# Gate sums of an xLSTM layer in three pieces instead of four, with the third gate move an iteration later

## The chip, the cores and the metric

The kernel runs on one core of a Trainium2 chip. The metric is the device time of one execution in microseconds; the median of three runs counts. The core's engines each work through a queue of their own in order: TensorE (PE, with its weight loads as PEld), VectorE (DVE), ScalarE (ACT), GpSimd (POOL) and SyncE (SP). SP and POOL also issue DMA transfers; an instruction that waits for one holds up everything behind it on its engine.

## The reference

The layer is an xLSTM cell (4 batches, 8 heads, 768 time steps, head size 40) and behind it a mixture of eight experts, of which each token takes two. Of the cell, the gates matter here:

```
m_new  = max(f[t] + m, i[t])          # a running maximum over the time steps
f_stab = exp(f[t] + m - m_new)
i_stab = exp(i[t] - m_new);  m = m_new
C = f_stab * C + i_stab * outer(v[t], k[t])
n = f_stab * n + i_stab * k[t]
y = sigmoid(o[t]) * (C @ q[t]) / max(|n . q[t]|, 1)
```

Then `x` (3072 tokens of 320) goes through the router (`x @ w_gate` plus scaled noise, the best two of eight, softmax) and through `relu(x @ w1[e]) @ w2[e]` for its two experts, weighted and added.

## The kernel before

The cell is computed in chunks of 64 time steps. A unit `u` is one chunk of one half of the batches, 16 pairs of batch and head at once; there are 24 units, and a loop over `i` (`while i < NU - LEAD`) runs over them, with parts of units `i`, `i + 1` and `i + 2` in one turn. The names used below, with `u` in brackets:

- `e(u)` (`e_part`, L347): TensorE multiplies the operands `LE` and `RE`, which hold the gates' sums, and ScalarE takes the exponential (L350): the decay matrix `w`. A pair of units reads one of two buffers of `LE` and `RE`.
- `s(u)` (L370, L367): scores of queries and keys; VectorE multiplies them with `w` to `p(u)` (L384).
- `kd(u)` (L378, VectorE): decayed keys; `c(u)` (L399, TensorE): the state for the next unit, taken out by ScalarE (L402).
- `o(u)` (L409, TensorE): the outputs; VectorE divides (L414, L416, L420, here called the division), POOL multiplies with the o gate (L421). `t(u)` (L432) transposes the result for the router.

In turn `i` TensorE's order is `c(i)`, `o(i)`, `t(i-1)`, `e(i+2)`, `s(i+2)`; for `i` below 2 the halves of `e` stand around. VectorE's order in a turn is `kd(i+1)`, the division of `o(i)`, `p(i+1)`, then some steps of the gates' sums. At a turn's start SP and POOL issue the loads of unit `i + 3` into one of four buffers (SP: q and k, half of v, the o gates; POOL: the other half of v), and POOL the store of unit `i - 1` (L424).

The gates' sums are made by `gate_math(t0, t1)`, eight VectorE instructions per piece of time steps: the scan of the running maximum (L230), an addition and a subtraction (L233, L235), a second scan within each chunk (L240), two subtractions (L242, L244), and two writes of the rounded sums and their rests into `HL` (L247, L249). Pieces 0 to 128 and 128 to 256 are made ahead of the loop. The others come from one generator, `gates2`, of which `gates_on(n)` takes the next `n` steps: `GATES[0]` ahead of the loop, two in its preparation, and `GATES[i + 1]` at the end of turn `i`, for `i` of 0 to 5. The gates themselves come in transfers: 256 to 512 by POOL early (L219), 512 and up by SP (L801), behind the loads of units 2 and 3.

`gate_move(kk)` issues three transfers that copy the sums of 128 time steps out of `HL` into a buffer of `LE` (L258) and `RE` (L260, two). Move `kk` serves units `2 kk` and `2 kk + 1` of the first half of the batches. Moves 0 to 2 stand ahead of the loop; the others at the start of even turns, move 3 at `i = 2`, move 4 at `i = 4`, on POOL's queue while `i < XV = 13`.

## Time and profile before

| | us |
|---|---|
| median of three runs (498.49 to 502.42) | 498.79 |
| the profiled execution | 500.44 |
| its span in the trace | 498.6 |

The profiled execution lies 1.65 us above the median, and 1.84 us of it lie around the span. Times in the rows are microseconds from the span's start. A row of a timeline has start, duration, engine, line, operation and tiles; what stands in square brackets is the engine's idle time before it and what ended that. "SPq" is SP's queue of transfers, where the row tells the issue and not the landing. [...]

### The profile page before, as it was taken

The numbers are of one execution on the slowest core, as the hardware profiler recorded it, in microseconds if no ns is written. First come the engines' busy times: TensorE is split into PE (matmuls) and PEld (weight loads), VectorE is DVE, ScalarE is ACT, GpSimd is POOL, SyncE is SP. The second block draws the span as 40 slices with busy tenths as digits, with TensorE's granted clock in tenths as the row PEclk, the third lists the DMA queues.
The fourth block names the chain that finished last, engine by engine and source line by source line (L and its number), as shares of the span: only waits on it lengthen the run. The fifth ranks groups of instructions, "written<-read, shape, count | busy, mean of one in ns | idle before, by whom it ended". The sixth has DMA issues, their size and how long they took to land.

```text
span 498.6 us, 14463 instructions
## 1 busy us (share of the span) xinstructions
PE 480.0 (96%) x5706; PEld 446.9 (90%) x5706; DVE 332.0 (67%) x900; ACT 248.6 (50%) x604; POOL 234.9 (47%) x303
## 2 busy tenths in 40 slices
PE   8988999898999999999999999999999999999995
PEld 3666877777999999999999999999999999999995
DVE  7886988859589866695964566285637548554511
ACT  7786888779664243463551444063424605513400
POOL 9765676255502574828238406801850480143043
PEclk9999999989999999999999999999999999999998
DMA  5899798886699775869489429916971991672033
GB/s 166 233 269 236 209 256 220 215 226 216 197 345 285 142 174 134 195 135 279 100 168 279 107 55 223 246 26 139 259 136 29 213 264 25 149 170 37 3 37 44
DMA packets 65082, 85.27 MB, mean 171 GB/s; under 512 B 12950, under 2 KB 53275, under 8 KB 64976
## 3 DMA queue, kind: packets, MB, share of 16 engines
q1 hardware_dynamic: 52640, 59.95, 46.1%
q0 software_dynamic: 12368, 24.33, 22.5%
q8 instruction: 47, 0.77, 0.7%
q14 instruction: 27, 0.22, 0.2%
HBM read 53.18 MB, written 17.28 MB: 141 GB/s over the span
## 4 chain that ended last, share of the span: by engine, by line
PE 81%; DVE 7%; DMA 3%; POOL 3%; ACT 2%; issue 2%; SPq 1%; POOLq 0%; ACTq 0%; DVEq 0%
PE s L1121 19%; PE e L1121 9%; PE o L1181 6%; PE o L1183 5%; PE o L1182 5%; PE s L1135 5%; PE st L1181 5%; PE st L1183 4%; PE st L1182 4%; PE o L409 3%; DMA qk<-qk_in 2%; PE s L370 2%; PE e L1135 2%; PE s L1259 1%; PE st L399 1%
## 5 line engine op out<-in xcount | busy, mean ns | idle before, releaser
L1205 POOL DMA_INDIRECT y_out<-y,tok x53 | 87.9, 1659 | 155.5 <-DVE y L1195 145.0
L1159 ACT ACTIVATE hx<-s 128x384 fp32r<-128x384 f32 (+3 forms) x86 | 39.5, 495 | 76.5 <-PE s L1121 61.7
L1162 DVE SCALAR_TENSOR_TENSOR hx<-s,hx 128x384 fp32r<-128x384 f32 (+1 forms) x86 | 45.4, 548 | 42.3 <-ACT hx L1159 39.5
L860 POOL DMA_INDIRECT xg<-rows,tok x53 | 59.3, 1119 | 27.1 <-issue 13.7
L1181 PE MATMUL o<-w2h,hx 128*128 128x320 f32 (+1 forms) x184 | 57.1, 311 | 0.0
L1183 PE MATMUL o<-w2h,hx 128*128 128x320 f32 (+1 forms) x184 | 56.7, 308 | 0.0
L1182 PE MATMUL o<-w2l,hx 128*128 128x320 f32 (+1 forms) x184 | 56.7, 308 | 0.0
L1181 PE MATMUL st<-w2h,hx 128*128 128x320 f32 x152 | 47.4, 312 | 0.0
L1183 PE MATMUL st<-w2h,hx 128*128 128x320 f32 x152 | 46.9, 308 | 0.0
L1182 PE MATMUL st<-w2l,hx 128*128 128x320 f32 x152 | 46.8, 308 | 0.0
L370 PEld LDWEIGHTS s<-qk 64*64 64x64 f32 x768 | 25.3, 136 | 14.0 <-issue 9.7
L1121 PE MATMUL s<-xh,w1h 64*128 64x384 f32 (+3 forms) x350 | 37.5, 341 | 0.0
L1121 PE MATMUL s<-xl,w1h 64*128 64x384 f32 (+3 forms) x350 | 37.2, 339 | 0.0
L421 POOL TENSOR_TENSOR raw<-tm,vk 128x320 f32<-128x320 f32 x24 | 21.1, 878 | 33.8 <-ACT w L350 7.5
L1121 PE MATMUL s<-xh,w1l 64*128 64x384 f32 (+3 forms) x350 | 36.9, 337 | 0.0
L356 ACT ACTIVATE vk<-vk 128x320 f32<-128x320 f32 x72 | 33.8, 471 | 4.3 <-DMA vk<-og_in 3.3
L1181 PEld LDWEIGHTS o<-w2h,hx 128*128 128x128 f32 (+1 forms) x184 | 34.4, 187 | 0.8 <-issue 0.8
L1094 ACT ACTIVATE xh<-xt__124 128x384 fp32r<-128x384 f32 (+1 forms) x60 | 27.1, 529 | 15.9 <-DMA xt__124<-xb 12.5
L1195 DVE TENSOR_SCALAR y<-o,gw 128x320 f32<-128x320 f32 x22 | 12.1, 551 | 33.8 <-PE o L1183 31.8
L1182 PEld LDWEIGHTS o<-w2l,hx 128*128 128x128 f32 (+1 forms) x184 | 34.4, 187 | 0.0
L1183 PEld LDWEIGHTS o<-w2h,hx 128*128 128x128 f32 (+1 forms) x184 | 34.3, 187 | 0.0
L370 PE MATMUL s<-qk 64*64 64x64 f32 x768 | 29.3, 223 | 3.8 <-issue 2.3
(327 smaller groups left out, 1319.6 us busy)
## 6 DMA issues: line engine op xcount, KB each, us to landing
raw<-w_in SPq DMA_DIRECT2D x16, 640.0 KB
raw<-w_in SPq DMA_DIRECT2D x7, 1280.0 KB
xt__124<-xb SPq DMA_DIRECT2D x72, 120.0 KB
qk<-qk_in SPq DMA_DIRECT2D x24, 256.0 KB
y_out<-zrow SPq DMA_DIRECT2D x15, 320.0 KB
vk<-vk_in POOLq DMA_DIRECT2D x24, 162.0 KB
vk<-vk_in SPq DMA_DIRECT2D x24, 162.0 KB
vk<-og_in SPq DMA_DIRECT2D x24, 160.0 KB
```

The costliest lines, as they stand in the source:

```text
L356: A.activation(g, g, (AF.Exp, AF.Ln, AF.Exp)[p], bias=float(p == 1), scale=(-1.0, 1.0, -1.0)[p])
L370: T.matmul(SQ[u][:, p][half[p], h, :], q[r, 1, h, :], q[r, 0, h, :], start=True, stop=True)
L860: P.indirect_dma_start(out=XG[0:rows_of(e, t), t], out_offset=None, in_=XD[0:n], in_offset=bass.IndirectOffsetOnAxis(ap=token(e, t), axis= ...
L1094: A.activation(fh(XH5[:, k]), fx(XT[:, k]), AF.Copy)
L1121: T.matmul(ps[y][:, 0:n], a[r, k, s], x[r, k, c], start=i == 0, stop=i == len(ops) - 1)
L1135: T.matmul(ps[:, 0:n], l, r, start=i == 0, stop=i == len(ops) - 1)
L1159: A.activation(hi, x, AF.Relu)
L1162: V.scalar_tensor_tensor(lo, top[0], 0.0, top[1].bitcast(F32), op0=OP.max, op1=OP.subtract)
L1181: T.matmul(ps[0:n], HH[:, j, c], W2H[:, j], start=j == 0, stop=False)
L1182: T.matmul(ps[0:n], HH[:, j, c], W2L[:, j], start=False, stop=False)
L1183: T.matmul(ps[0:n], HLO[:, j, c], W2H[:, j], start=False, stop=j == 7)
L1205: apart(e, P.indirect_dma_start(out=out, out_offset=bass.IndirectOffsetOnAxis(ap=token(e, t), axis=0), in_=y[0:n], in_offset=None, **(how ...
```

## The change

The four pieces of 128 time steps behind 256 become three: 256 to 384, 384 to 640 and 640 to 768. `GATES` spreads their 24 steps (32 before) over the turns: behind the eight ahead of the loop, three, three and two steps in turns 0 to 2 (the wide piece) and the same in turns 3 to 5. Gate move 3, for units 6 and 7, stands at the start of turn 3 instead of turn 2; the other moves stay.

```diff
-GATES = (6, 4, 4, 4, 4, 4, 4)
+GATES = (6, 3, 3, 2, 3, 3, 2)
...
-    gates2 = (s for t0 in range(256, S, 128) for s in gate_math(t0, t0 + 128))
+    gates2 = (s for t0, t1 in ((256, 384), (384, 640), (640, S)) for s in gate_math(t0, t1))
...
-        if i % 2 == 0 and i and i // 2 + 2 < 2 * GB:
-            gate_move(i // 2 + 2, (P, P) if i < XV else (SP, SP))
+        if i == 3 or i % 2 == 0 and i > 2 and i // 2 + 2 < 2 * GB:
+            gate_move(3 if i == 3 else i // 2 + 2, (P, P) if i < XV else (SP, SP))
```

VectorE's queue from the end of turn 0 into turn 1, before (`xg` holds the running maximum, `raw_119` the gates and scratch, `dn` and `tm` are the division; waits stand in square brackets, by the semaphore's name):

```order
L384 TENSOR_TENSOR p<-s,w 128x1024
L230 SCALAR_TENSOR_TENSOR xg<-raw_119,xg 64x128
L233 TENSOR_TENSOR raw_119<-raw_119,xg 64x128 [waits DVE_49]
L235 TENSOR_TENSOR raw_119<-raw_119,xg 64x128 [waits DVE_49]
L240 SCALAR_TENSOR_TENSOR xg<-raw_119 64x128 [waits DVE_49]
L378 TENSOR_TENSOR kd<-vk_111,w 128x640 [waits DMASW6_49,DMAHW0_49,Activation_49,Pool_49]
L414 RECIPROCAL dn<-o 128x8 [waits PE_49]
```

The same place of the changed kernel:

```order
L384 TENSOR_TENSOR p<-s,w 128x1024
L230 SCALAR_TENSOR_TENSOR xg<-raw_119,xg 64x256 [waits DMAHW2_49]
L233 TENSOR_TENSOR raw_119<-raw_119,xg 64x256 [waits DVE_49]
L235 TENSOR_TENSOR raw_119<-raw_119,xg 64x256 [waits DVE_49]
L378 TENSOR_TENSOR kd<-vk_111,w 128x640 [waits DMASW6_49,DMAHW0_49,Activation_49,Pool_49]
L414 RECIPROCAL dn<-o 128x8 [waits PE_49]
```

The scan is twice as wide, waits for a transfer of SP's (DMAHW2), and kd(2) stands behind it as before; the second scan has gone to the end of turn 1. Before, a scan with that wait stood two turns later.

SP's queue of transfers at that time, the same in both kernels (`qk`, `vk` with `vk_in` and `vk` with `og_in` are a unit's loads, `raw_119<-fi_in` the gates of 512 and up, L801):

```order
L192 DMA vk_112<-og_in 128x320 [waits DMAHW1_49]
L801 DMA raw_119<-fi_in 64x2x256 [waits DMAHW2_49]
L802 DMA xt__124<-wgn_in 128x96 [waits DMAHW3_49]
L185 DMA qk_105<-qk_in 64x1024 [waits DMAHW4_49]
L185 DMA qk_105<-qk_in 16x1024 [waits DMAHW5_49]
L190 DMA vk_109<-vk_in 64x648 [waits DMAHW6_49,PE_49]
L192 DMA vk_109<-og_in 128x320 [waits DMAHW7_49,Pool_49]
L185 DMA qk_106<-qk_in 64x1024 [waits DMAHW0_49]
L185 DMA qk_106<-qk_in 16x1024 [waits DMAHW1_49]
L190 DMA vk_110<-vk_in 64x648 [waits DMAHW2_49,DVE_49,PE_49]
```

Eight semaphores go round: each transfer waits until the one eight places ahead, on its own semaphore, has landed. The last row's transfer, `vk_110` for unit 5, is the next on DMAHW2 behind the gates of L801.

POOL's queue around the third gate move (`le_100` and `re_98` are its targets, L421 the product with the o gate, L190 and L424 a unit's load and store), as a difference:

```order
+L421 TENSOR_TENSOR raw_123<-tm,vk_111 128x320
+L190 DMA vk_111<-vk_in 64x648
+L424 DMA rows<-raw_123 128x320
 L258 DMA le_100<-hl 32x2x64
 L260 DMA re_98<-hl 1x16x128 x2
-L421 TENSOR_TENSOR raw_123<-tm,vk_111 128x320
-L190 DMA vk_111<-vk_in 64x648
-L424 DMA rows<-raw_123 128x320
```

The move stood ahead of the product, load and store of turn 2 and stands behind them now.

## Rows read from the trace of the kernel before

**Rows 1.** The page: the chain that ended last, by engine.

```profile
PE 81%; DVE 7%; DMA 3%; POOL 3%; ACT 2%; issue 2%; SPq 1%; POOLq 0%; ACTq 0%; DVEq 0%
```

**Rows 2.** The chain, pieces in order of time: start us, us, what.

```profile
13.42 4.83 DMA vk<-og_in
...
24.85 7.67 DMA qk<-qk_in
```

**Rows 3.** Table of windows: length, busy us (instructions) per engine, PEclk, DMA share, GB/s.

```profile
24.00:30.00 6.00, 5.18 (x161) 4.45 (x155) 5.65 (x14) 5.73 (x14) 4.53 (x8) 1.00 0.93 254
```

**Rows 4.** Timeline, SP's issues: the first gates, o gates, the late gates, vk.

```profile
0.74 0.70 SPq L208 DMA_DIRECT2D raw<-fi_in  x1
...
13.42 1.26 SPq L192 DMA_DIRECT2D vk<-og_in  x2
...
19.56 0.63 SPq L801 DMA_DIRECT2D raw<-fi_in  x1
...
25.55 0.54 SPq L190 DMA_DIRECT2D vk<-vk_in  x1
```

**Rows 5.** Timeline, VectorE: the first scan, then turns 0 to 4.

```profile
3.20 0.48 DVE L230 TENSOR_TENSOR_SCAN xg<-raw,xg 64x128 f32<-64x128 f32 x1 [0.59 <-DMA raw<-fi_in]
...
18.39 0.47 DVE L230 TENSOR_TENSOR_SCAN xg<-raw,xg 64x128 f32<-64x128 f32 x1
...
21.92 0.21 DVE L414 RECIPROCAL dn<-o 128x8 f32<-128x8 f32 x1 [0.54 <-PE o L409]
...
23.91 0.28 DVE L242 TENSOR_TENSOR xg<-raw,xg 64x128 f32<-64x128 f32 x1
...
24.54 0.29 DVE L247 CAST hl<-xg 64x256 fp32r<-64x256 f32 x1
24.86 0.48 DVE L249 SCALAR_TENSOR_TENSOR hl<-hl,raw,xg 64x256 fp32r<-64x256 f32 x1
25.26 0.81 DVE L378 TENSOR_TENSOR kd<-vk,w 128x640 f32<-128x640 f32 x1
...
35.59 0.21 DVE L414 RECIPROCAL dn<-o 128x8 f32<-128x8 f32 x1 [0.64 <-PE o L409]
```

**Rows 6.** Timeline, TensorE: o(2), e(4), o(3), s(5), o(4), e(6), rest of s(6).

```profile
24.41 1.10 PE L409 MATMUL o<-vk,p 128*64 128x41 f32 x32
...
26.82 0.50 PE L347 MATMUL st<-re,le 98*128 98x512 f32 x1 [0.82 <-ACT vk L402]
...
29.20 1.23 PE L409 MATMUL o<-vk,p 128*64 128x41 f32 x32
...
32.66 0.27 PE L370 MATMUL s<-qk 64*64 64x64 f32 x2 [1.28 <-DMA qk<-qk_in]
...
34.38 1.13 PE L409 MATMUL o<-vk,p 128*64 128x41 f32 x32
...
35.75 0.48 PE L347 MATMUL st<-re,le 98*128 98x512 f32 x1
...
38.26 0.59 PE L367 MATMUL s<-qk,cs 64*64 64x512 f32 x1 [0.78 <-issue]
```

**Rows 7.** Timeline: SP's issue in the first gate move, and its reader e(0).

```profile
7.22 0.59 SPq L260 DMA_DIRECT2D re<-hl  x1
...
10.32 0.47 PE L347 MATMUL e<-re,le 98*128 98x512 f32 x1 [0.47 <-DMA re<-hl]
```

**Rows 8.** Timeline, POOL: the last two issues of gate move 3.

```profile
26.58 0.99 POOL L260 DMA_DIRECT2D re<-hl  x2
```

**Rows 9.** Chain at two turns of the router's matmuls, and a window between 99 and 100.

```profile
79.05 0.79 PE st L465 x24
...
96.00 1.15 issue
...
98.95 1.38 PE st L465 x24
...
99.00:100.00 1.00, 1.00 (x24) 0.88 (x21) 0.84 (x4) 0.23 (x1) 0.00 (x0) 0.50 0.68 242
```

## The prediction

> **What bounds the kernel now.** I read the page first: TensorE makes up 81% of the chain that ended last, so a microsecond lost on TensorE early is, as a rule, a microsecond at the end [rows 1]. The change touches only the first seven turns of the attention loop (i = 0 to 6, about 15 to 50 us), so I then read those from the chain, the table of windows and each engine's timeline. Two things are to be seen there. First, the chain passes twice through a transfer that SP issued long before: 4.83 us from the issue of the o gates to their landing, and 7.67 us for the tiles of unit 5 [rows 2]. Second, between 24 and 30 us VectorE is busy for 5.65 of 6 us, more than TensorE with 5.18 [rows 3]; it leads there. By 35.6 us that has turned: VectorE waits 0.64 us for TensorE's output [rows 5], and from then on TensorE leads, with a stop of 0.78 us before 38.26 in which it waits for nothing that the profile shows [rows 6].

> **What the change removes.** Two pieces of 128 columns become one of 256: eight instructions fewer, same columns. In turns 4 to 6 the steps left out lie in VectorE's wait for TensorE and are worth nothing; if that cover went, they are worth at most the eight durations themselves, 0.28 to 0.48 each and 2.8 us in all [rows 5], less what the wider ones take more. In turns 0 to 3, where VectorE leads, I count each step as it now stands. A scan of 128 columns took 0.47 us and an addition 0.28; at 256 columns they lie between that and twice that, so I take the middle, 0.70 and 0.42, as an estimate from those rows.

> **What it moves, first: a wait into VectorE's queue.** The scan at the end of turn 0 now covers 384 to 640. So it reads gates of 512 and up, which SP issues only at 19.56 [rows 4]. Before, that wait (DMAHW2 in the order's rows) stood two turns later, by when the gates had long landed (below). The scan of before began at 18.39 [rows 5], before the issue; it must now wait. When does the transfer land? Not before 19.56 + 2.46 = 22.0: 2.46 us is what the very first gates took from issue (0.74) to the scan that waited for them (3.20), with an empty queue [rows 4, 5]. Not after 25.55: SP's next transfer on the same semaphore waits for it, and is issued then [rows 4]. Between them I go by the nearest row, the second o gate of the pair at 13.42: the two issues take 1.26 us, so the second starts at about 14.05, and the pair has landed by 18.25 [rows 2, 4], which is 4.2 us. 19.56 + 4.2 = 23.8, and that is also the middle of the bounds. [...]

> So VectorE stands still from 18.39 to 23.8, 5.4 us. Behind the scan in its queue stand two more steps, then kd(2) and p(2) with the division for unit 1 between them, and TensorE waits for these.

> **From there to TensorE, step by step** (after against before):
> - The three steps, 0.70 + 0.42 + 0.42 and small gaps, end at 25.4. Then kd(2), 0.8, and the division and p(2), which took from 21.92 to 23.91, 2.0 [rows 5]: p(2) is ready at 28.2, and o(2) starts at 28.3 instead of 24.41: 3.9 late [rows 6].
> - e(4) stood 0.82 us waiting for ScalarE before [rows 6]; ScalarE is done long before now, so that is eaten: e(4) and s(4) are 3.1 late.
> - VectorE still leads: from 28.2 three wide steps 1.6, kd(3) 0.8, division and p(3) 2.0: 32.6. o(3) starts at 32.7, against 29.20 [rows 6]: 3.5 late.
> - s(5) waited 1.28 us for the tiles of unit 5 until 32.66 [rows 6]. Their issue on SP hangs on nothing that is late, so this too is eaten: 3.5 - 1.3 = 2.2 late.
> - From 32.6 the two last steps, now 512 columns wide, between 0.77 (0.29 + 0.48) and 1.54 [rows 5]: I take 1.25, 33.9. kd(4), division and p(4) take 2.8 more: o(4) at 36.8, against 34.38 [rows 6]: 2.5 late.

> **What it moves, second: the third gate move.** It leaves POOL's queue at i = 2 and stands at i = 3, behind POOL's product, load and store of unit 2. Before, POOL issued its last two transfers at 26.58, some 9 us ahead of e(6), its reader, at 35.75 [rows 6, 8]. Now it waits for the steps that end at 33.9; its three issues take about 0.5 each [rows 8], the last from 35.0 on. POOL's later loads and stores of unit 3 lie behind it, but its product of unit 3 comes after p's division at about 35.5 anyway, so they lose nothing. e(6) would come at 35.75 + 2.5 = 38.25. The nearest row for a landing is the first gate move, issued 7.22, waited for until 10.32: 3.1 us with little in the queues [rows 7]. The far end is 7.67 us [rows 2]. Landing is thus between 38.1 and 42.7; by the 4.2 us taken above it is 39.2, 0.95 after e(6) wants it. Part of that lies beside the 0.78 us stop in s(6) [rows 6], which TensorE need not have a second time; I count 0.5.

> **Sum.** +3.9 (o(2)) - 0.8 (ScalarE's wait eaten) + 0.4 (VectorE leads at o(3)) - 1.3 (DMA wait eaten) + 0.3 (VectorE at o(4)) + 0.5 (gate move) = +3.0 us. Behind turn 6 nothing is edited, and TensorE stays the leader, so I carry it to the end. Against the profiled execution's 500.44 us that is 503.4; the median of the runs is 498.79, 1.65 us lower, and on its scale I predict **501.8**. With a landing at 22.0 and a gate move in time, the own range of this case begins at 500.3; at 25.55 it ends at 503.5.

> **The rivals.**
> - **Absorbed.** The gates land at 22.0: VectorE is 3.6 late, o(2) 2.1, e(4) 1.3; VectorE leads at o(4) with 0.7, the gate move is in time, and the 0.78 us stop swallows most of the rest: +0.5, 499.3. For it speak the 2.46 us and that TensorE has three waits to be eaten in these turns [rows 6]; against it the loaded queue.
> - **The gate move decides: slower by over 1%.** If its landing takes the 7.67 us of rows 2, e(6) starts 4.4 late and, less 0.8 beside the stop, the sum is 2.5 + 3.6 = +6.1: 504.9. It passes 1% once landing takes more than 6.5 us from the last issue (net 2.5). For it: the DMA engines are at 0.93 from 24 to 30 us [rows 3], and the move stands behind a load and a store in POOL's queue. Against it: while VectorE stands still, POOL's product of unit 1 and the load and store behind it aren't issued, so the queues run emptier.
> [...]
> - **It gains.** If no wait arose, the fewer steps would give at most half of the 2.8 us, as the wider ones take half as long again: 1.4, so 497.4. That needs the gates to be there at 18.39, before their issue at 19.56. I keep 0.02 for what I have not seen.

> **How the numbers follow.** Main case 0.50, absorbed 0.15, clock 0.15, gate move 0.18, gain 0.02. About 1% (5 us) is what a measurement of this kernel can tell from no change; slower than that are most of the gate move's case and the upper edges of the main and clock cases, together 0.22; faster by over 1% hardly anything, 0.02; the rest, 0.76, is within 1%. The range 499.0 to 505.0 holds the main and clock cases, half of the absorbed one and over half of the gate move's.

> **What would show it.** Right: VectorE's row before the 256 wide scan carries 5 us of idle time, released by the gates' transfer, near 23.8; o(2) near 28.3; the 1.28 us wait of s(5) and ScalarE's 0.82 gone; e(6) with a wait of about 1 us for the gate move. Wrong: a scan that starts near 22 or 25.5, a clock of 0.5 between 27 and 35 us, an e(6) later than 40, or a lateness at c(7) that is no longer there at the loop's end, which would say that TensorE is not the leader in between.

## The result, and the profile after

The changed kernel took 501.0 us (median of 20 runs, 497.92 to 504.83) against 498.02 us for the kernel before (median of 20 runs beside them, 495.58 to 503.46). The ratio is **1.0083, with a 95% interval of 1.0062 to 1.0104**: a loss that is measured, but within the 1% that the forecast calls no change. This ratio leaves out executions in a slower state, and it is not the quotient of the medians, which is 1.0060, or of the means of all runs (501.25 and 498.68), which is 1.0051. So the loss is about 4.1 us by the ratio (3.1 to 5.2 by its interval), 3.0 by the medians and 2.6 by the means; that there is one is clear, its size only within these. The forecast was 501.8 us.

Single runs of one kernel spread by 7 to 8 us here, twice the effect, so the two profiled executions can't size it: that of before took 500.44 us, 2.4 above its median, that of after 501.40 us, 0.4 above its own, and their spans differ by 1.0 us alone (498.6 and 499.6). What the pair of traces does show is where each step came to stand.

VectorE in the profile of after, the turns 0 to 4 (timeline: start us, length us, engine, line, what it does; in brackets the idle time before it and what ended it):

```profile
24.17 0.74 DVE L230 TENSOR_TENSOR_SCAN xg<-raw,xg 64x256 f32<-64x256 f32 x1 [5.89 <-DMA raw<-fi_in]
24.95 0.42 DVE L233 TENSOR_TENSOR raw<-raw,xg 64x256 f32<-64x256 f32 x1
...
25.75 0.81 DVE L378 TENSOR_TENSOR kd<-vk,w 128x640 f32<-128x640 f32 x1
...
32.72 0.41 DVE L247 CAST hl<-xg 64x512 fp32r<-64x512 f32 x1
33.17 0.74 DVE L249 SCALAR_TENSOR_TENSOR hl<-hl,raw,xg 64x512 fp32r<-64x512 f32 x1
...
35.83 0.21 DVE L414 RECIPROCAL dn<-o 128x8 f32<-128x8 f32 x1 [1.19 <-PE o L409]
```

The scan that stood at 18.39 without a wait [rows 5] now stands still for 5.89 us for the late gates' transfer. SP issues that transfer where it did before, at 19.45 against 19.56 [rows 4]; SP's timeline of after has the row

```profile
19.45 0.64 SPq L801 DMA_DIRECT2D raw<-fi_in  x1
```

so it had landed 4.7 us after its issue began. The two steps at 512 columns take 0.41 and 0.74, and by 35.83 VectorE waits for TensorE again, 1.19 us: TensorE leads from there, as before.

TensorE in the profile of after, same columns: c(2), o(2), e(4), o(3), first products of s(5), o(4), e(6), o(5), o(6):

```profile
26.66 1.25 PE L399 MATMUL st<-vk,kd 104*40 104x41 f32 x32 [2.91 <-issue]
28.68 1.94 PE L409 MATMUL o<-vk,p 104*64 104x41 f32 x32 [0.77 <-DVE p L384]
...
31.10 0.78 PE L347 MATMUL st<-re,le 98*128 98x512 f32 x1
...
34.65 1.10 PE L409 MATMUL o<-vk,p 104*64 104x41 f32 x31
...
36.63 0.27 PE L370 MATMUL s<-qk 64*64 64x64 f32 x2
...
38.35 1.13 PE L409 MATMUL o<-vk,p 128*64 128x41 f32 x32
...
39.72 0.48 PE L347 MATMUL st<-re,le 98*128 98x512 f32 x1
...
42.65 1.13 PE L409 MATMUL o<-vk,p 104*64 104x41 f32 x32
...
47.10 1.10 PE L409 MATMUL o<-vk,p 104*64 104x41 f32 x31
```

The stop of 2.91 us ahead of c(2) has no releaser in its row, but c(2) reads kd(2), and that ends at 25.75 + 0.81 = 26.56 in the rows above. Two more things are to be seen. The stops of before are gone: ScalarE's 0.82 ahead of e(4), the 1.28 for the tiles of unit 5 ahead of s(5), and the 0.78 in s(6) [rows 6]; e(6) waits for nothing. And the 32 matmuls of o(2) took 1.94 us where they took 1.10 before [rows 6]. The table of windows of after says why (length, busy us and instructions of PE, PEld, DVE, ACT, POOL, then PEclk, the granted clock of TensorE as a share of its full speed, the DMA share, GB/s):

```profile
24.00:27.00 3.00, 0.34 (x13) 0.37 (x15) 2.69 (x7) 1.68 (x4) 0.00 (x0) 0.96 0.81 266
27.00:30.00 3.00, 2.23 (x53) 2.12 (x50) 2.97 (x6) 1.24 (x3) 1.91 (x3) 0.50 0.52 107
30.00:33.00 3.00, 3.00 (x33) 2.27 (x35) 2.82 (x6) 1.52 (x4) 1.17 (x2) 0.50 0.91 284
33.00:36.00 3.00, 3.00 (x96) 2.88 (x88) 1.78 (x4) 1.96 (x5) 2.34 (x5) 0.90 0.84 210
```

TensorE did 0.34 us of work between 24 and 27, and from 27 to 33 the granted clock stood at 0.50; before it was 1.00 from 24 to 30 [rows 3], and up to 36 too. Between 30 and 33 TensorE is busy for all 3.00 us: there the clock, not VectorE, sets the pace.

Set side by side, in us (the start of the first of the matmuls that a row names; o(3) has one matmul of its own at 34.60, ahead of the row above):

| step | before | forecast | after | late |
|---|---|---|---|---|
| late gates landed | no wait | 23.8 | 24.17 | |
| o(2) | 24.41 | 28.3 | 28.68 | 4.3 |
| e(4) | 26.82 | 29.9 | 31.10 | 4.3 |
| o(3) | 29.20 | 32.7 | 34.60 | 5.4 |
| s(5) | 32.66 | 34.9 | 36.63 | 4.0 |
| o(4) | 34.38 | 36.8 | 38.35 | 4.0 |
| e(6) | 35.75 | 39.2 | 39.72 | 4.0 |
| o(6), 31 of its matmuls | 46.50 | 49.5 | 47.10 | 0.6 |

The last row is no gain of the change. In the trace of before TensorE stops for nothing shown, 0.78 us in s(6) [rows 6] and once more in s(7) (here, and wherever a row ends in `<-issue`, the profile names nothing that it waited for); the timeline of before has there, and at o(6):

```profile
44.75 0.21 PE L370 MATMUL s<-qk 64*64 64x64 f32 x1 [1.32 <-issue]
...
46.50 1.10 PE L409 MATMUL o<-vk,p 104*64 104x41 f32 x31
```

After has neither stop. Experiments 5 and 6 below have such stops too, and the last section says where in TensorE's program they stand.

Where the loop's lateness ends is told by the first matmul behind the attention loop (instructions of one line, times each: shortest, median and longest ns, first and last start in us). Before, and after:

```profile
L1135 PE MATMUL s<-xl,w1h x80: 332/342/443, 129.5 to 190.3; 128*128 128x384 f32 x50, 128*128 128x416 f32 x30
```

```profile
L1135 PE MATMUL s<-xl,w1h x80: 331/343/449, 130.3 to 191.1; 128*128 128x384 f32 x50, 128*128 128x416 f32 x30
```

From there to the end of the span before takes 498.6 - 129.5 = 369.1 us and after 499.6 - 130.3 = 369.3. All profiled executions of this study lie between 369.0 and 370.1 here. So what the kernels and executions differ by arises ahead of about 130 us, and is carried to the end to within 1.1 us.

### The profile page after: what moved, and what is told of

It reads as the page before. It is cut to its first block, busy times and chain, and to the rows that moved or that the text cites. A ratio compares the mean times of both kernels' runs of the same rounds, so it can differ in the third digit from the quotient of the medians.

```text
span 499.6 us, 14450 instructions
## 1 busy us (share of the span) xinstructions
PE 480.2 (96%) x5703; PEld 449.0 (90%) x5706; DVE 330.9 (66%) x892; ACT 248.3 (50%) x604; POOL 233.7 (47%) x303
## 4 chain that ended last, share of the span: by engine, by line
PE 85%; DVE 6%; ACT 4%; issue 2%; DMA 1%; SPq 1%; POOL 0%; POOLq 0%; ACTq 0%; DVEq 0%
PE s L1121 19%; PE e L1121 9%; PE o L1181 5%; PE o L1183 5%; PE o L1182 5%; PE s L1135 5%; PE st L1181 5%; PE st L1183 4%; PE st L1182 4%; PE o L409 4%; PE s L370 3%; PE st L399 2%; PE xt L432 2%; PE e L1135 2%; PE s L1259 1%
## 5 line engine op out<-in xcount | busy, mean ns | idle before, releaser
L1162 DVE SCALAR_TENSOR_TENSOR hx<-s,hx 128x384 fp32r<-128x384 f32 (+1 forms) x86 | 45.3, 547 | 42.7 <-ACT hx L1159 37.9
L860 POOL DMA_INDIRECT xg<-rows,tok x53 | 59.2, 1117 | 29.8 <-issue 13.4
L421 POOL TENSOR_TENSOR raw<-tm,vk 128x320 f32<-128x320 f32 x24 | 21.0, 874 | 34.8 <-DVE tm L420 10.7
L1094 ACT ACTIVATE xh<-xt__124 128x384 fp32r<-128x384 f32 (+1 forms) x60 | 27.1, 528 | 16.2 <-DMA xt__124<-xb 13.4
L1121 PEld LDWEIGHTS s<-xh,w1h 64*128 64x128 f32 x350 | 31.0, 185 | 1.4 <-issue 1.1
```

What stands on the lines that cost most here:

```text
L860: P.indirect_dma_start(out=XG[0:rows_of(e, t), t], out_offset=None, in_=XD[0:n], in_offset=bass.IndirectOffsetOnAxis(ap=token(e, t), axis= ...
L1094: A.activation(fh(XH5[:, k]), fx(XT[:, k]), AF.Copy)
L1121: T.matmul(ps[y][:, 0:n], a[r, k, s], x[r, k, c], start=i == 0, stop=i == len(ops) - 1)
L1162: V.scalar_tensor_tensor(lo, top[0], 0.0, top[1].bitcast(F32), op0=OP.max, op1=OP.subtract)
```

## The experiments

Theory A, that of the forecast: the late gates' wait at the head of VectorE's queue makes the loss, and the rest of the change is nearly free. The rivals: the third gate move makes it (B), the fallen clock makes it (C), or the wider pieces themselves do (D). Each run below undoes or does one of these. Ratios are to the kernel before in runs beside it, taken as above (its medians there: 499.21 us for the first four, 498.60 for the next four, 499.42 for the last two).

**1. The wait undone in the changed kernel.** POOL's early transfer of the second gates takes all the rest of them, and SP's late one goes:

```
-    P.dma_start(fit[:, :, 256:512], fi[:, :, 256:512])
+    P.dma_start(fit[:, :, 256:], fi[:, :, 256:])
...
-    SP.dma_start(fit[:, :, 512:], fi[:, :, 512:])
```

> The changed kernel with one thing undone: the gates of 512 and up come with those of 256 to 512 in POOL's one early transfer (256 KB instead of 128), so that the wide scan at the end of turn 0 has nothing to wait for; SP's later transfer of them is gone. Pieces, steps and the third gate move stay as changed. Theory 1 (the wait in VectorE's queue is what costs): no idle time ahead of the wide scan, o(2) back near 24.5 us, granted clock 1.00 through 24 to 36 us, ratio to the kernel before 0.996 to 1.002. Rival (the later gate move, or the wide pieces, cost): ratio still 1.006 or more although the wait is gone.

Measured: 501.43 us, ratio 1.0051 (1.0020 to 1.0082). The wait is gone, and TensorE's timeline of this kernel shows what came in its place:

```profile
25.13 1.10 PE L409 MATMUL o<-vk,p 128*64 128x41 f32 x32
...
33.66 1.13 PE L409 MATMUL o<-vk,p 128*64 128x41 f32 x32
...
38.14 0.47 PE L347 MATMUL st<-re,le 98*128 98x512 f32 x1 [2.87 <-DMA re<-hl]
...
39.42 1.07 PE L370 MATMUL s<-qk 64*64 64x64 f32 x16
```

o(2) is at 25.13 instead of 28.68, o(4) at 33.66 instead of 38.35. But e(6) now stands still for 2.87 us, waiting for the third gate move, whose last two issues POOL's timeline has at

```profile
30.88 0.98 POOL L260 DMA_DIRECT2D re<-hl  x2
```

The second of the two starts at about 31.37, so it needed 6.8 us to land. Behind that stop TensorE ran slower: the 16 products of s at 39.42 took 1.07 us, against 0.63 at 32.45 in the same trace, where the clock was 1.00 (24 to 36 us); in the trace of after 16 of them took 1.06 at 32.39, with the clock at 0.50. The ratio expected was missed, and the rival's 1.006 or more wasn't reached either. What follows: B is real, but hidden in the changed kernel, where TensorE came 4 us late to e(6) and found the move landed. Two costs lie beside each other and the later one counts; undoing one uncovers the other. On the time alone this run doesn't separate A from B, as its interval overlaps that of the changed kernel.

**2. The wait done alone, in the kernel before.** One copy of one column of the late gates on VectorE, behind turn 0 and ahead of its gate steps:

```
+        if i == 0:
+            V.tensor_copy(rmt[:, 256:257], fit[:, 0, 512:513])
         if i < 6:
```

> The kernel before with one instruction more: ahead of the gate steps at the end of turn 0 VectorE copies one column of the gates of 512 and up to scratch, and so waits for their transfer at the place where the changed kernel does. Pieces and gate moves are those of before. Theory 1: 5 to 6 us of idle time ahead of the copy, the clock at 0.50 for a stretch behind it, ratio 1.005 to 1.012, as the changed kernel. Rival (move or pieces): ratio 0.998 to 1.003, the stall is swallowed by waits that TensorE has anyway.

Measured: 502.96 us, ratio **1.0086** (1.0056 to 1.0115). VectorE's timeline, then TensorE's:

```profile
24.61 0.15 DVE L985 COPY raw<-raw 64x1 f32<-64x1 f32 x1 [6.20 <-DMA raw<-fi_in]
```

```profile
27.06 0.82 PE L399 MATMUL st<-vk,kd 104*40 104x41 f32 x32 [2.57 <-issue]
29.08 1.94 PE L409 MATMUL o<-vk,p 104*64 104x41 f32 x32 [1.20 <-DVE p L384]
```

A copy of 0.15 us brings the whole picture of the changed kernel: the wait of 6.20 us, the stop ahead of c(2), o(2) at 1.94 us. Pieces and gate moves are those of before. What follows: the wait suffices for the whole loss (A); B and D are not needed. Its first matmul behind the loop comes at 133.9 (in an execution of 504.73 us, 1.8 above this kernel's median):

```profile
L1137 PE MATMUL s<-xl,w1h x80: 331/343/444, 133.9 to 194.7; 128*128 128x384 f32 x50, 128*128 128x416 f32 x30
```

**3. The third gate move an iteration later, alone, in the kernel before.**

```
-        if i % 2 == 0 and i and i // 2 + 2 < 2 * GB:
-            gate_move(i // 2 + 2, (P, P) if i < XV else (SP, SP))
+        if i == 3 or i % 2 == 0 and i > 2 and i // 2 + 2 < 2 * GB:
+            gate_move(3 if i == 3 else i // 2 + 2, (P, P) if i < XV else (SP, SP))
```

> The kernel before with only the third gate move put a turn later (start of turn 3). Theory 1: it has slack, e(6) waits for nothing, ratio 0.998 to 1.002. Rival (the move costs): its transfers land 4 to 8 us after their issue near 29 to 30 us, e(6) near 35.8 us waits for them, ratio 1.003 or more.

Measured: 499.53 us, ratio 1.0018 (0.9987 to 1.0048): no cost is shown, and one above half a per cent is excluded. TensorE's timeline:

```profile
33.13 0.27 PE L370 MATMUL s<-qk 64*64 64x64 f32 x2 [2.11 <-DMA qk<-qk_in]
...
37.15 0.47 PE L347 MATMUL st<-re,le 98*128 98x512 f32 x1 [0.68 <-ACT raw L436]
```

e(6) waits for ScalarE, not for the move. In this order the wait for the tiles of unit 5, 2.11 us, stands ahead of it and covers the landing.

**4. The clock held up in the changed kernel.** Eleven matmuls of 128x512 on data that nobody reads, ahead of c(2), where TensorE stands idle; they add work and leave none out:

```
         st = psum.tile([128, 512], F32, name="st")
+        if u == 2:
+            warm(11, st)
```

> The changed kernel with 11 dummy matmuls (128x512, bf16, their result is overwritten) ahead of c(2), in TensorE's stop of 2.9 us. The stall of VectorE stays. If the fall of the clock is a good part of the price: granted clock 1.00 from 24 to 36 us, o(3) about 1.3 us earlier than the changed kernel's 34.7, and a ratio to before of 1.002 to 1.006 instead of 1.008. If the clock's fall lies beside VectorE's lead: ratio as the changed kernel's, 1.006 to 1.010.

Measured: 503.02 us, ratio 1.0087 (1.0062 to 1.0113), so no gain. The windows of this kernel, then its e(6):

```profile
24.00:36.00 12.00, 9.25 (x209) 6.98 (x209) 10.81 (x23) 7.15 (x18) 5.30 (x9) 1.00 0.73 216
```

```profile
41.74 0.47 PE L347 MATMUL st<-re,le 98*128 98x512 f32 x1 [2.89 <-DMA re<-hl]
```

The clock was 1.00 from 24 to 36, and o(3) came at 33.35 instead of 34.60. But e(6) then waited 2.89 us for the gate move, whose last issue POOL began at about 35.65: 6.1 us to its landing. Behind this second stop TensorE ran slower after all: 16 products of s took 1.06 us at 42.69, against 0.63 at 31.73. Again the second cost stood under the first. So this run leaves open what the clock costs; experiment 9, where the move is in time, is the test of it.

**5. Both undone: early gates, and the third move back at its place,** with the steps of the wide piece spread so that they are done in time (`GATES = (6, 4, 4, 0, 4, 4, 0)`).

> The changed kernel with POOL's one early transfer for all late gates (as early_gates), the wide piece's steps four and four in turns 0 and 1, and the third gate move back at turn 2. Theory 2 (formed on early_gates: with the wait gone, the late writes of the wide piece and the later move make e(6) wait for the move's landing): no wait for it at e(6), ratio 1 to 4 thousandths under early_gates' 1.005, that is 1.001 to 1.004, as before_early. Rival (the early transfer is what costs in early_gates): ratio stays at 1.005 and before_early's is the same.

Measured: 500.76 us, ratio 1.0031 (0.9996 to 1.0066). The waits for gates and move are gone, and stops that wait for nothing shown stand in their place:

```profile
36.60 0.59 PE L367 MATMUL s<-qk,cs 64*64 64x512 f32 x1 [0.83 <-issue]
...
44.13 0.21 PE L370 MATMUL s<-qk 64*64 64x64 f32 x1 [2.36 <-issue]
```

By the middle of the interval most of the loss is gone, though the interval leaves both nothing and two thirds of a per cent. (The execution profiled is this kernel's slowest, 503.81 us.) Three things could make the rest: the early transfer, the wide pieces, or chance. The next three runs take them one by one.

**6. The early transfer alone, in the kernel before** (the edit of experiment 1).

> The kernel before with only POOL's one early transfer of all late gates in place of the two. It measures that transfer by itself: in early_gates' trace o(0) started at 17.0 us instead of 15.5. Theory 2: 1.000 to 1.003. Rival (the early transfer costs): 1.004 or more.

Measured: 498.98 us, ratio 0.9989 (0.9961 to 1.0016). It costs nothing that can be measured. The expectation rests on o(0) in the trace of experiment 1, which came at 16.71 there, against 15.20 before; here it comes at 15.14. The same stops are there:

```profile
42.12 0.21 PE L370 MATMUL s<-qk 64*64 64x64 f32 x1 [1.93 <-issue]
...
49.24 0.57 PE L370 MATMUL s<-qk 64*64 64x64 f32 x13 [2.30 <-issue]
```

So those stops come with kernels that lose nothing, and are no mark of the change.

**7. The wait undone another way:** the late gates stay on SP, but are issued ahead of the k tiles of unit 3; third move and steps as in experiment 5.

```
     load_unit(1, "g")
+    SP.dma_start(fit[:, :, 512:], fi[:, :, 512:])
     load_unit(3, "k")
```

> The changed kernel with SP's transfer of the late gates put ahead of the tiles of unit 3 (issue near 14.8 us instead of 19.5), four and four steps and the third gate move at turn 2. By the 4.2 to 4.9 us that a transfer took here it lands at 19 to 19.7, so the scan waits 0.7 to 1.5 us. Theory 2: nothing of the change costs any more, ratio 0.997 to 1.003, faster than the changed kernel by 0.5% or more. Rival (wide pieces cost by themselves): 1.005 or more.

Measured: 499.88 us, ratio 1.0039 (1.0003 to 1.0075). VectorE's timeline, and TensorE's:

```profile
18.93 0.74 DVE L230 TENSOR_TENSOR_SCAN xg<-raw,xg 64x256 f32<-64x256 f32 x1 [0.71 <-DMA raw<-fi_in]
```

```profile
24.72 1.13 PE L410 MATMUL o<-vk,p 104*64 104x41 f32 x32 [0.41 <-DVE p L385]
...
29.51 0.90 PE L410 MATMUL o<-vk,p 104*64 104x41 f32 x24 [0.37 <-DVE p L385]
```

A wait of 0.71 us instead of 5.89 leaves o(2) and o(3) 0.3 late (in this kernel's fastest execution, 494.64 us). The ratio lies above the 1.003 that was expected at most. As in experiment 5 some three or four tenths of a per cent seem to stay, with an interval that all but touches nothing.

**8. Wide pieces alone:** the kernel before with the last two pieces as one of 256 columns (512 to 768), whose first step comes when those gates have long landed, and `GATES = (6, 4, 4, 4, 4, 0, 0)`.

```
-    gates2 = (s for t0 in range(256, S, 128) for s in gate_math(t0, t0 + 128))
+    gates2 = (s for t0, t1 in ((256, 384), (384, 512), (512, S)) for s in gate_math(t0, t1))
```

> The kernel before with the wide piece at the end: 256 to 384, 384 to 512, 512 to 768, steps 4, 4, 4, 4 in turns 0 to 3 and none in turns 4 and 5, gate moves as before. As many instructions as the changed kernel, but no earlier wait and no later move. Theory: the eight instructions saved lie in VectorE's wait for TensorE, the wider ones take about 0.8 us more in turns 2 and 3; ratio 0.998 to 1.003. Rival (wide pieces cost): 1.005 or more; (they gain): under 0.997.

Measured: 499.82 us, ratio 0.9994 (0.9956 to 1.0031). Eight instructions fewer bring nothing that is measured, and the wider ones cost nothing either: D falls as the cause of the loss, and so does the gain. The wide piece stands in turns 2 and 3 here, not in 0 to 2.

**9 and 10. The wait alone with and without the clock,** on one chip: experiment 2 with the eleven idle matmuls of experiment 4 ahead of c(2), and experiment 2 again.

> The kernel before with the wait of wait_alone (one copy that waits for the late gates at the end of turn 0) and the 11 dummy matmuls of after_warm ahead of c(2). The third gate move stands at turn 2, so that it can't be late here, as it was in after_warm's trace (e(6) waited 2.9 us for it). If the fall of the clock is a good part of the wait's price: granted clock 1.00 from 24 to 36 us, o(3) about 1 us earlier than wait_alone's 35.5, ratio 1.003 to 1.006. If it lies beside VectorE's lead: 1.007 to 1.011, as wait_alone.

> wait_alone once more, for the comparison with wait_warm on the same chip: ratio 1.006 to 1.011.

Measured: 503.46 us, ratio 1.0069 (1.0032 to 1.0105) with the matmuls, just between the two ranges expected, and 502.91 us, 1.0078 (1.0045 to 1.0112) without. Windows and TensorE's timeline of the first:

```profile
24.00:36.00 12.00, 10.42 (x234) 7.87 (x234) 11.23 (x27) 8.40 (x19) 5.41 (x9) 1.00 0.83 231
```

```profile
23.85 2.55 PE L784 MATMUL st<-xt__124 128*128 128x512 bf16 x10
...
28.30 1.13 PE L411 MATMUL o<-vk,p 104*64 104x41 f32 x32 [1.15 <-DVE p L384]
...
32.62 1.13 PE L411 MATMUL o<-vk,p 104*64 104x41 f32 x32 [0.38 <-DVE p L384]
```

The windows of the second (0.58 is its mean clock), and its wait:

```profile
24.00:36.00 12.00, 7.62 (x128) 6.67 (x130) 10.14 (x24) 5.28 (x12) 5.41 (x9) 0.58 0.66 196
```

```profile
25.24 0.15 DVE L985 COPY raw<-raw 64x1 f32<-64x1 f32 x1 [6.90 <-DMA raw<-fi_in]
```

With the clock at 1.00, o(3) comes at 32.62, against 35.23 in the trace of experiment 2, 2.6 us sooner, 0.8 of it already at o(2). Over the twelve executions of each, the mean granted clock was 0.992 with the matmuls and 0.987 without, against 0.9925 for the kernel before beside them. So the matmuls gave the clock back, and yet a loss stays that is clear of nothing, and the time is not shown to be better than without them (the profiled execution, 498.35 us, is this kernel's fastest). C is therefore not the whole loss. The second run repeats the main finding: one wait, 1.0078 after 1.0086.

## Why the prediction was right, and where it was not

**Where the time goes: right, and shown.** The forecast put the loss down to the scan's wait for gates that SP issues at 19.56. That wait alone, in the kernel before, gives 1.0086 and 1.0078, the changed kernel 1.0083. Wide pieces alone, at a later place (0.9994), and the early transfer alone (0.9989) give nothing that is measured; the move alone (1.0018) is not told from nothing.

**The landing: right.** 23.8 was said, with bounds of 22.0 and 25.55; it was 24.17, and 24.6 and 25.2 in experiments 2 and 10. The choice of the loaded queue's 4.2 us [rows 2, 4] against the empty queue's 2.46 held: 4.7 us. The DMA share was 0.93 from 19.45 to 24.17 in the trace of after, 0.94 from 13.4 to 18.25 in that of before, where the 4.2 us come from, and 0.27 from 0.74 to 3.20, where the 2.46 do.

**The wide steps: right.** 0.70, 0.42 and 1.25 for the last two were estimated; 0.74, 0.42 and 0.41 + 0.74 = 1.15 were measured. The middle between once and twice the narrow step is a fair price for the double width here.

**o(2) and the waits eaten: right.** 28.68 against 28.3. ScalarE's 0.82 and the 1.28 for the tiles of unit 5 are gone, as said.

**The clock: the step that failed.** The forecast gave a fall of the clock a chance of 0.15, and its sum has nothing for it. The stop that the change makes is 2.91 us ahead of c(2), with 0.77 ahead of o(2) behind it, and the clock was 0.50 from 27 to 33 us. The trace of before has such a pattern later on (a clock of 0.50 from 99 to 100, behind a stop of 1.15 us at 96.0, and 1.38 us for 24 matmuls that took 0.79 [rows 9]), but also a stop of 1.28 us ahead of 32.66 [rows 6] with a clock of 1.00 up to 36. The chance was too low. A clock of 0.5 between 27 and 35 us is also among the signs of being wrong that the forecast names. o(3) came at 34.60 instead of 32.7, o(4) at 38.35 instead of 36.8; 0.4 us of each was there at o(2), from the later landing. What the clock did is read from pairs with the same wait: from o(2) to o(3) it took 5.9 us here and 6.15 in experiment 2 with the fallen clock, 4.15 in experiment 4 and 4.3 in experiment 9 with matmuls in the stop, which kept the clock at 1.00. That is 1.8 us, and the fall came of TensorE's stop here: the clock was 0.50 behind it and 1.00 where matmuls filled it.

**The gate move: right for this kernel, for a reason that was not given.** About 1 us of waiting was said, 0.5 of it counted; there was none. POOL's timeline of after has the last two issues in one row, the second from about 35.25, and e(6) at 39.72 waited for nothing, so it landed within 4.5 us:

```profile
34.76 0.98 POOL L260 DMA_DIRECT2D re<-hl  x2
```

But the fallen clock had a part in that: without the move e(6) was forecast at 38.25, 1.5 us sooner than it came. Where TensorE came sooner (experiments 1 and 4), the landing took 6.8 and 6.1 us, which is close to the 6.5 us from which this rival decides. Its price was sized fairly; that it lies under the other cost, and so adds nothing to it, was left out. The forecast added 0.5 for it.

**The stop in s(6): half right.** The forecast let TensorE keep half of the 0.78 us. In the trace of after neither this stop nor that of 1.32 us in s(7) is there, which gives back 1.7 and 1.6 us (o(5) is 2.2 late, o(6) 0.6). The 0.78 is less than the stop costs: s(6) as a whole takes 2.9 us before, from 36.39 on, and 1.15 after. Experiments 5 and 6 have such stops of 0.83 to 2.36 us, so a late TensorE may lose less of its time there than an early one; that is argued from the traces (last section), not shown by an experiment.

**The size: near, in part by luck.** +3.0 us was forecast. The medians give +3.0, the means +2.6, the ratio +4.1 (3.1 to 5.2), so by the ratio the sum is short by about a microsecond, by the others it isn't. The lateness at o(4) and e(6) was 4.0 us in the traces, against 2.5 and 3.5 forecast: the sum leaves out the clock's fall, and it adds 0.5 for a wait for the gate move that didn't come. That the end lies near the forecast all the same is luck as far as these two go. How much of the lateness lasts to 130 us the traces can't say: in this pair it is 0.2 at c(7) and 0.8 at 130 us, but the two executions of the kernel with the wait alone (experiments 2 and 10) differ there by 2.4 us, 133.9 and 131.5.

**A bound that doesn't follow.** The lower end of the main case, 500.3, isn't what the forecast's own steps give: a landing 1.8 us sooner and no wait for the gate move leave 3.0 - 1.8 - 0.5 = +0.7 us, 499.5 on its scale. The whole range holds that as well, and no reading above hangs on it.

**Still open.** What the fallen clock costs at the end: 1.0069 with it held up, 1.0078 and 1.0086 without, and the intervals overlap. Whether the changed kernel without wait and late move is still slower: 1.0031 and 1.0039, intervals that reach down to 0.9996 and 1.0003. No version here beat the kernel before.

## What to carry to other kernels

When a step is moved ahead or widened, look for every transfer that it reads, where that is issued, and what stands behind the step in its engine's queue: here one instruction of 0.74 us held up a whole engine for 5.9 us, and one copy of 0.15 us did the same. Costs that lie beside each other don't add up: undoing one shows the next, so a part counts as free only where it was done alone on the kernel before, and as the whole cause only where it alone gives the whole loss. And one pair of traces tells where steps stand, not a difference of 1%, when single runs spread by 7 us.
